# First batch's k rectified on VectorE, its transposes copied by ScalarE, epsilon added by TensorE; block 0's attends a slot up

## The chip, the cores and the metric

The kernel runs on one core of one Trainium2 chip. The metric is the device time of one execution in microseconds (us). The profile counts its own clock from the first to the last instruction (the span), which is about 1.7 us less than the run time here: the profiled run of the kernel before took 988.33 us for a span of 986.6. All stretches below are microseconds from the start of the span.

## The reference

Linear attention with a cosine feature map, followed by a layer of eight gated experts. Only the attention matters for this change.

```python
# q, k, v: 8 batches x 8 heads x 576 positions x 64
q_p = phi(q, cos_w, sin_w)      # relu(x)*cos and relu(x)*sin, side by side: 128 features
k_p = phi(k, cos_w, sin_w)
kv  = einsum('bhsf,bhsd->bhfd', k_p, v)
z   = sum(k_p, axis=2)
num = einsum('bhsf,bhfd->bhsd', q_p, kv)
den = einsum('bhsf,bhf->bhs', q_p, z)[..., None] + 1e-06
x   = num / den                 # then 4608 x 512 into the experts:
out = sum over e of P[:, e] * (relu(x @ w1[e]) @ w2[e])   # P: 8 rounds of normalised gates
```

## The kernel before

Each batch goes through these stages: rectify q and k, multiply them by the table (`q_p`, `k_p`), transpose `q_p` (batches 0 and 1 by TensorE, later ones by DMA), sum `kv` and `z`, form the denominators and their reciprocals, and "attend", which multiplies and writes the batch's part of `xT`. The first expert's two matmuls run in blocks of 512 tokens of 16 slots each (8 for `w1`, 8 for `w2`). The next batch's attention work is queued behind chosen slots with `at(block, slot, ...)`. In the traces VectorE runs its instructions in the order in which they are written. Dummy matmuls (`keep_busy`) fill TensorE's time before the first real work.

```python
qp_pool = tile_pool(name="qp_pool", bufs=3)      # the q_p buffers
rb_pool = tile_pool(name="rb_pool", bufs=4)      # reciprocals spread over partitions, for attend
# ... (cut)
def keep_busy(n):
    for _ in range(n):
        te.matmul(out=idle_ps[:, 0:P], lhsT=ones_sq[:], rhs=ones_sq[:], start=True, stop=True)

def prep_k(b, hk):
    k16 = loaded["k", b, hk]
    se.activation(out=k16, in_=k16, func=AF.Relu)

def prep_q(b, hk):
    q16 = loaded.pop(("q", b, hk))
    by_dma = b >= 2
    if by_dma:
        ve.tensor_scalar(out=q16, in0=q16, scalar1=0.0, scalar2=None, op0=ALU.max)
    q_p = qp_pool.tile([P, C, 2, D], F16, name="q_p")
    ve.tensor_tensor(out=q_p[:], in0=q16..., in1=cs, op=ALU.mult)
    if by_dma:
        qTs[b, hk] = q_pTs[(b * HK + hk) % len(q_pTs)]
        nc.sync.dma_start(out=qTs[b, hk], in_=q_p..., transpose=True)
    else:
        qps[b, hk] = q_p
# ... (cut: prep_kp makes k_p on VectorE, prep_v copies v, turn transposes on TensorE,
#      sums_begun is the kv matmuls, sums_made reads them into kv_sb and zsel)
def denominators(b):
    den_ps = ps_s.tile([P, 512], FP32, name="small_ps")
    # ... 24 matmuls zsel x q_pT into den_ps
    ve.tensor_scalar(out=den[:], in0=den_ps[0:96, 0 : C3 * HP], scalar1=1e-6 / XS, ..., op0=ALU.add)
    ve.reciprocal(out=den[:], in_=den[:])
    # ... hi and lo parts into hl, which attend spreads by matmuls
# ... (cut) the start:
for hk in range(HK):
    prep_q(0, hk)
    for i in range(3):
        turn(0, hk, i, hk < 2 or i != 1)         # True: copied by ScalarE, False: by VectorE
for hk in range(HK):
    prep_k(0, hk)
    prep_kp(0, hk)
keep_busy(30)
for half in range(2):
    prep_v(0, 2 * half, se.copy)
    prep_v(0, 2 * half + 1, ve.tensor_copy)
    begun.append(sums_begun(0, half))
    keep_busy((16, 6)[half])
sums_made(0, 0, begun[0])
sums_made(0, 1, begun[1])
denominators(0)
keep_busy(34)
# ... (cut) block 0's schedule: denominators of batch 1 at slot 9, its attends at 12 to 15,
#     batch 2's q and k preparation at 11 to 15, batch 2's last q and k at block 1
```

## Time and profile before

| | us |
|---|---|
| median of 3 runs | 986.7 (986.63 to 988.38) |
| span of the profiled run | 986.6 |
| TensorE busy | 969.7, 98% of the span |
| first attend of batch 0, 1, 2 starts at | 22.18, 43.45, 63.20 |

From the page: the span, and the first table, in which PE is TensorE, DVE VectorE, ACT ScalarE and POOL GpSimd, each with its busy time, its share of the span and its instructions.

```profile
span 986.6 us, 20264 instructions
...
PE 969.7 (98%) x7864; PEld 678.5 (69%) x7864; DVE 808.1 (82%) x1833; ACT 568.1 (58%) x1266; POOL 60.4 (6%) x82
```

TensorE is full. What there is to win lies in the first 60 us, where TensorE waits, runs dummies, or runs at half clock. The timeline of the start shows start, duration, engine, line, operation, tiles and count, and in brackets the idle time before with what ended it:

```profile
12.36 2.39 ACT L109 ACTIVATE k_ld<-k_ld 128x576 f16<-128x576 f16 x4
...
13.06 2.77 DVE L109 TENSOR_TENSOR k_p<-k_ld,acc_hi 128x1152 f16<-128x1152 f16 x4 [0.85 <-ACT k_ld L109]
...
15.36 0.46 PE L109 MATMUL small_ps<-acc_lo,k_p 64*128 64x65 f16 x18 [0.60 <-ACT acc_lo L109]
...
17.64 0.74 PE L109 MATMUL small_ps<-acc_lo,k_p 64*128 64x65 f16 x36
...
18.76 0.84 PE L109 MATMUL small_ps<-q_pT,zsel 128*32 128x192 f16 x24
19.64 0.35 DVE L109 TENSOR_SCALAR den<-small_ps 96x192 f32<-96x192 f32 x1 [0.87 <-PE small_ps L109]
20.03 1.35 DVE L109 RECIPROCAL den<-den 96x192 f32<-96x192 f32 x1
...
22.18 0.42 PE L109 MATMUL small_ps<-hl,acc_hi 96*128 96x192 f16 x3 [0.58 <-DVE hl L109]
```

Read from the top: ScalarE rectifies k late because it copies transposes first, VectorE follows with `k_p`, the kv sums (`acc_lo,k_p`) follow that, then the denominators (`zsel`), epsilon, the reciprocal, and the first attend (`hl,acc_hi`) at 22.18. The second loss is at the head of block 1, in the timeline around 50 us:

```profile
49.06 0.82 PE L109 MATMUL h_ps<-xT,w1e 128*128 128x512 f16 x3
...
50.76 0.81 DVE L109 TENSOR_TENSOR xT<-small_ps,rb 128x384 f16<-128x384 f32 x2
51.62 2.19 PE L109 MATMUL h_ps<-xT,w1e 128*128 128x512 f16 x5 [1.74 <-DVE xT L109]
...
53.75 1.17 PE L109 MATMUL small_ps<-acc_lo,k_p 64*128 64x65 f16 x36
...
63.20 0.41 PE L109 MATMUL small_ps<-hl,acc_hi 96*128 96x192 f16 x3
```

The first matmuls of block 1 wait 1.74 us for `xT`, which stands on VectorE behind work for batch 2. What comes after is slow: 36 kv sums take 1.17 us, against 0.74 in the start. The first attend of batch 2 is the line at 63.20. The table of stretches gives the reason. After each stretch's limits and length come, by engine, busy time and instructions, then the granted clock of TensorE (1.00 is full), the DMA share and GB/s:

```profile
48.33:51.74 3.41, 1.67 (x12) 0.72 (x10) 3.38 (x9) 1.77 (x4) 0.00 (x0) 1.00 1.25 163
51.74:55.15 3.41, 3.41 (x42) 1.59 (x41) 2.87 (x6) 1.39 (x4) 0.00 (x0) 0.50 1.02 205
```

The whole stretch of 3.41 us after the stall runs at half clock. The view of TensorE's waits over the first 110 us puts `xT` first:

```profile
PE h_ps L109 <- DVE xT L109: 1.9, 2, 1.7
```

### The profile page before, as it was taken

To read this page: it belongs to the slowest core of one execution; us is meant where nothing else is said; L and a number is where in the kernel's file an instruction comes from. 1 tells how busy PE (TensorE), PEld (TensorE's weight loads), DVE (VectorE), ACT (ScalarE), POOL (GpSimd) and SP (SyncE) were. 2 spreads that over 40 slices of the span, in tenths; PEclk is the share of its full clock that TensorE was granted. 3 is DMA by queue.
4 is the path that set the end of the run, shared out by engine and by line. 5 is a ranking of instruction groups with operands and counts; after the bars stand their busy time and mean duration, and the time that the engine had idled before them with its cause. 6 is when DMAs were issued, how large, how long until landed. Compare 5 with 4: busy or idle time off the path is not lost.

```text
span 986.6 us, 20264 instructions
## 1 busy us (share of the span) xinstructions
PE 969.7 (98%) x7864; PEld 678.5 (69%) x7864; DVE 808.1 (82%) x1833; ACT 568.1 (58%) x1266; POOL 60.4 (6%) x82
## 2 busy tenths in 40 slices
PE   8999999989999999999999999999999999999997
PEld 7544545447777777777777777777777777777775
DVE  6776774789889888988789888988789888988887
ACT  5756665467776555555555555555555555555551
POOL 6312110010000000000000000000000000000001
PEclk9999999999999999999999999999999999999999
DMA  9979990642013410133113400233103400104435
GB/s 166 206 108 153 160 153 20 127 75 60 26 49 68 80 36 25 41 76 68 45 29 67 92 25 26 51 65 68 49 25 67 92 25 27 48 26 114 130 86 129
DMA packets 80336, 73.54 MB, mean 75 GB/s; under 512 B 33264, under 2 KB 72176, under 8 KB 80240
## 3 DMA queue, kind: packets, MB, share of 16 engines
q0 software_dynamic: 27232, 30.94, 20.0%
q1 hardware_dynamic: 52768, 41.06, 17.1%
q8 instruction: 61, 1.00, 0.4%
q14 instruction: 35, 0.29, 0.1%
q10 hardware_dynamic: 240, 0.26, 0.1%
HBM read 83.12 MB, written 12.98 MB: 97 GB/s over the span
## 4 chain that ended last, share of the span: by engine, by line
PE 93%; DVE 3%; ACT 1%; DMA 1%; issue 1%; POOL 0%; DVEq 0%; ACTq 0%; SPq 0%; POOLq 0%
PE rows_ps L109 34%; PE h_ps L109 28%; PE copied_ps L109 11%; PE p_ps L109 11%; PE y_ps L109 5%; PE small_ps L109 4%; DMA q_pT<-q_p 1%; DVE k_p L109 0%; DVE xT L109 0%; DVE acc_hi L819 0%; POOL hs_last L834 0%; DVE P_tok L109 0%; DMA out_dram<-acc_lo 0%; ACT q_pT L109 0%; DVE colp L109 0%
## 5 line engine op out<-in xcount | busy, mean ns | idle before, releaser
L819 DVE SCALAR_TENSOR_TENSOR acc_lo<-rows_ps,P_tok,acc_lo 128x512 f32<-128x512 f32 (+1 forms) x322 | 203.4, 641 | 74.4 <-PE rows_ps L109 74.3
L109 PEld LDWEIGHTS <-H 128*128 128x128 f16 x2080 | 203.0, 98 | 83.1 <-issue 1.2
L755 ACT CAST u<-h_ps 128x384 f16<-128x384 f32 x288 | 137.8, 478 | 131.1 <-PE h_ps L109 131.1
L109 PEld LDWEIGHTS <-w1e 128*128 128x128 f16 x1632 | 156.4, 98 | 68.5 <-issue 9.0
L749 DVE CUSTOM_DVE_ANT_0 H<-p_ps,u 128x384 f16<-128x384 f32 x329 | 181.3, 551 | 6.5 <-PE p_ps L109 6.3
L109 PEld LDWEIGHTS <-hs 128*128 128x128 f16 x1500 | 146.6, 98 | 56.2
L109 PE MATMUL h_ps<-S,w1e 128*128 128x384 f16 x672 | 164.1, 326 | 1.1 <-ACT u L109 0.9
L109 PE MATMUL p_ps<-xT,T 128*128 128x384 f16 x672 | 164.1, 326 | 0.1
L109 PE MATMUL h_ps<-xT,w1e 128*128 128x384 f16 (+1 forms) x616 | 151.4, 353 | 1.9 <-DVE xT L109 1.9
L109 PE MATMUL rows_ps<-V,H 128*128 128x256 f16 x1000 | 150.0, 273 | 0.7 <-DVE acc_hi L819 0.7
L109 PE MATMUL rows_ps<-w2e,hs 128*128 128x256 f16 x1000 | 150.0, 273 | 0.0
L787 ACT ACTIVATE H<-h_ps 128x384 f16<-128x384 f32 x144 | 70.7, 491 | 95.0 <-PE h_ps L109 95.0
L109 PEld LDWEIGHTS <-T 128*128 128x128 f16 x1008 | 98.1, 98 | 29.5 <-issue 3.1
L109 PE MATMUL rows_ps<-w2e,H 128*128 128x256 f16 (+1 forms) x568 | 91.2, 285 | 0.0
L768 ACT COPY copied_ps<-h_ps 128x384 f32<-128x384 f32 x144 | 67.5, 468 | 35.4 <-PE h_ps L109 35.4
L778 ACT ACTIVATE H<-copied_ps 128x384 f16<-128x384 f32 x144 | 70.9, 492 | 20.3 <-PE copied_ps L109 20.3
L109 PE MATMUL h_ps<-S,T 128*128 128x384 f16 x336 | 81.8, 325 | 0.4 <-ACT copied_ps L109 0.3
L109 PE MATMUL copied_ps<-xT,w1e 128*128 128x384 f16 x336 | 82.1, 326 | 0.0
L109 PE MATMUL copied_ps<-w2e,H 128*128 128x256 f16 x504 | 75.5, 272 | 0.0
L109 PE MATMUL rows_ps<-V,hs 128*128 128x256 f16 x500 | 75.0, 272 | 0.0
L819 DVE SCALAR_TENSOR_TENSOR acc_lo<-copied_ps,P_tok,acc_lo 128x256 f32<-128x256 f32 x126 | 60.2, 478 | 0.6 <-PE copied_ps L109 0.2
L819 DVE SCALAR_TENSOR_TENSOR acc_hi<-rows_ps,P_tok,acc_hi 128x512 f32<-128x512 f32 (+1 forms) x56 | 41.3, 738 | 20.5 <-PE rows_ps L109 19.7
(135 smaller groups left out, 957.1 us busy)
## 6 DMA issues: line engine op xcount, KB each, us to landing
S<-x_saved SPq DMA_DIRECT2D x108, 192.0 KB, 2.4
out_dram<-acc_lo SPq DMA_DIRECT2D x62, 128.0 KB, 2.4
w1e<-in_moe_w_dram POOLq DMA_DIRECT2D x7, 1024.0 KB, 9.1
w2e<-in_moe_w_dram POOLq DMA_DIRECT2D x7, 1024.0 KB, 10.0
q_ld<-in_q_dram POOLq DMA_DIRECT2D x16, 288.0 KB, 7.7
k_ld<-in_k_dram POOLq DMA_DIRECT2D x16, 288.0 KB, 8.8
v_ld<-in_v_dram POOLq DMA_DIRECT2D x16, 288.0 KB, 10.0
x_saved<-S SPq DMA_DIRECT2D x18, 192.0 KB, 1.8
```

The costliest lines, as they stand in the source:

```text
L109: i = getattr(self.engine, name)(*args, **kwargs)
L749: latest = ve._custom_dve(TENSOR_ADD_SAT, out=out, in0=ps[:, 0:TU], in1=t[:], s0=FP32_MAX, s1=0.0)
L755: se.copy(out=t[:], in_=ps[:, 0:TU])
L768: se.copy(out=Y[:, 0:TU], in_=X[:, 0:TU])
L778: se.activation(out=h11, in_=Y[:, 0:TU], func=AF.Relu)
L787: se.activation(out=h12, in_=X[:, 0:TU], func=AF.Relu)
L819: ve.scalar_tensor_tensor(out=a, in0=rows, scalar=P_tok[:, g, self.e : self.e + 1], in1=a, op0=ALU.mult, op1=ALU.add,)
```

## The change

The intent has two parts. In the start, the first attend is to come earlier: VectorE rectifies batch 0's k as it lands, ScalarE copies all of batch 0's transposes, the first query load is issued ahead of an iota, epsilon goes into the denominators' accumulation by matmuls, and there are fewer dummies. In block 0, batch 1's attends move up a slot and part of batch 2's preparation moves to block 1, so that `xT` is in time.

```diff
+        load(0, 0, "q")
         nc.gpsimd.iota(gidx[:], ...)
-        load(0, 0, "q")
 ...
         def prep_k(b, hk):
             k16 = loaded["k", b, hk]
-            se.activation(out=k16, in_=k16, func=AF.Relu)
+            if b:
+                se.activation(out=k16, in_=k16, func=AF.Relu)
+            else:
+                ve.tensor_scalar(out=k16, in0=k16, scalar1=0.0, scalar2=None, op0=ALU.max)
 ...
+        def epsilons(b):       # three matmuls, start=True: eps_row x a row of ones into den_ps
 ...
-                turn(0, hk, i, hk < 2 or i != 1)
+                turn(0, hk, i, True)
 ...
-        keep_busy(30)
+        keep_busy(16)
         for half in range(2):
             prep_v(0, 2 * half, se.copy)
-            prep_v(0, 2 * half + 1, ve.tensor_copy)
+            prep_v(0, 2 * half + 1, (se.copy, ve.tensor_copy)[half])
             begun.append(sums_begun(0, half))
-            keep_busy((16, 6)[half])
+            keep_busy((4, 6)[half])
 ...
+        epsilons(0)
         denominators(0)        # for b == 0: no add on VectorE, the reciprocal reads PSUM
 ... block 0 (and its prep_q, turn, sums_made of batch 1 one or two slots earlier)
-                at(0, 9, denominators, 1)
-                at(0, 10, gates, 0)
+                at(0, 8, denominators, 1)
+                at(0, 9, gates, 0)
-                    at(0, 12 + hk, attend, 1, hk)
+                    at(0, 11 + hk, attend, 1, hk)
 ... block 1
-                    at(j, 0, prep_q, b, 3)
-                    at(j, 1, prep_kv, b, 3)
+                    for hk in (2, 3):
+                        at(j, 0, prep_q, b, hk)
+                        at(j, hk - 2, prep_kp, b, hk)
+                        at(j, hk - 2, prep_v, b, hk, se.copy)
 ... batch 2 in block 0: q 0 and 1, k_p 0 and 1 (v copied by ScalarE), all k rectified, slots 11 to 15
```

More of the change, by code (lines that the diff above doesn't have):

```diff
@@ L299 @@
         ve.memset(scale_row[:, 1, :], float(N) / float(E) / XS)
+        eps_row = cs_pool.tile([1, 32], FP32, name="eps_row")
+        ve.memset(eps_row[:], 1e-6 / XS)
         wg_ld = cs_pool.tile([P, KT, E], FP32, name="wg_ld")
@@ L430, in sums_made @@
                     values()
+        den_pss = {}
+        def epsilons(b):
+            den_pss[b] = ps_s.tile([P, 512], FP32, name="small_ps")
+            for j in range(3):
+                te.matmul(
+                    out=den_pss[b][32 * j : 32 * j + 32, 0 : C3 * HP],
+                    lhsT=eps_row[:],
+                    rhs=ones_col[0:1, :].to_broadcast([1, C3 * HP]),
+                    start=True,
+                    stop=False,
+                )
         def denominators(b):
             zsel = kvs[b][1]
-            den_ps = ps_s.tile([P, 512], FP32, name="small_ps")
+            den_ps = den_pss.pop(b, None)
+            if den_ps is None:
+                den_ps = ps_s.tile([P, 512], FP32, name="small_ps")
             for h in range(H):
@@ L442, in denominators @@
                         rhs=qTs[b, hk][:, j * C3 : (j + 1) * C3, hh * HP : (hh + 1) * HP],
-                        start=(h == 0),
+                        start=(h == 0 and b > 0),
                         stop=(h == H - 1),
@@ L446, in denominators @@
             den = kv_pool.tile([96, C3 * HP], FP32, name="den")
-            ve.tensor_scalar(
-                out=den[:], in0=den_ps[0:96, 0 : C3 * HP], scalar1=1e-6 / XS, scalar2=None,
-                op0=ALU.add,
-            )
-            ve.reciprocal(out=den[:], in_=den[:])
+            if b:
+                ve.tensor_scalar(
+                    out=den[:], in0=den_ps[0:96, 0 : C3 * HP], scalar1=1e-6 / XS,
+                    scalar2=None, op0=ALU.add,
+                )
+                ve.reciprocal(out=den[:], in_=den[:])
+            else:
+                ve.reciprocal(out=den[:], in_=den_ps[0:96, 0 : C3 * HP])
             hi = kv_pool.tile([96, C3 * HP], F16, name="hi")
@@ L565 @@
         prep_v(1, 3, ve.tensor_copy)
-        ahead = (
-            (prep_k, 0), (prep_q, 0), (prep_k, 1), (prep_kv, 0), (prep_q, 1), (prep_k, 2),
-            (prep_kv, 1), (prep_q, 2), (prep_k, 3), (prep_kv, 2),
-        )
         for j in range(B):
@@ L573 @@
             if j == 0:
+                at(0, 4, prep_q, 1, 0)
                 at(0, 4, lambda: begun.append(sums_begun(1, 0)))
@@ L577 @@
                 at(0, 5, lambda: begun.append(sums_begun(1, 1)))
-                at(0, 6, prep_q, 1, 0)
-                at(0, 6, lambda: sums_made(1, 1, begun[3]))
-                at(0, 6, prep_q, 1, 1)
+                at(0, 5, prep_q, 1, 1)
                 for hk in range(HK):
                     for i in range(3):
-                        at(0, 6 + hk, turn, 1, hk, i)
+                        at(0, 5 + hk, turn, 1, hk, i)
+                    if hk == 0:
+                        at(0, 5, lambda: sums_made(1, 1, begun[3]))
                     if hk < 2:
-                        at(0, 6 + hk, prep_q, 1, hk + 2)
-                at(0, 9, denominators, 1)
-                at(0, 10, gates, 0)
+                        at(0, 5 + hk, prep_q, 1, hk + 2)
+                at(0, 8, denominators, 1)
+                at(0, 9, gates, 0)
                 for hk in range(HK):
-                    at(0, 12 + hk, attend, 1, hk)
+                    at(0, 11 + hk, attend, 1, hk)
             elif b < B:
                 if j == 1:
-                    at(j, 0, prep_q, b, 3)
-                    at(j, 1, prep_kv, b, 3)
+                    for hk in (2, 3):
+                        at(j, 0, prep_q, b, hk)
+                        at(j, hk - 2, prep_kp, b, hk)
+                        at(j, hk - 2, prep_v, b, hk, se.copy)
                     at(j, 1, sums, b, 0)
@@ L605 @@
                     at(j, 3, load, b + 1, half)
-                for i, (fn, hk) in enumerate(ahead):
-                    at(j, 11 + i // 2, fn, b + 1, hk)
+                for slot, fn, hk, *args in (
+                    (11, prep_k, 0), (11, prep_q, 0), (12, prep_k, 1), (12, prep_kp, 0),
+                    (12, prep_v, 0, se.copy), (13, prep_q, 1), (14, prep_k, 2),
+                    (14, prep_kp, 1), (14, prep_v, 1, se.copy), (15, prep_k, 3),
+                ):
+                    at(j, slot, fn, b + 1, hk, *args)
             elif b + 1 < B:
```

## The prediction

> **What bounds it now.** The page has TensorE busy 98% of 986.6 us; from 100 us on the stretches table gives 877.4 busy of 886. The change touches the first 60 us. Idle there, by tens: 1.96, 1.82, 1.03, 0.59, 0.21, 1.62 us. Much "busy" before 24 us is dummy matmuls that keep the clock up, so the chain of waits prices the start: query load, transposes, k rectified on ScalarE from 12.36, four k_p on VectorE to 15.83, v copies, kv sums to 18.38, denominators to 19.6, VectorE add 0.39, reciprocal 1.36, first attend at 22.18.
> The second loss is at 49.9: block 1's first matmuls wait 1.74 us for xT, which stands on VectorE behind the third batch's work (9.08 us busy in 40-50). The granted clock is then 0.50 from 51.9 to 55.1, about 1.6 us more. [...]
>
> **What changes.**
> 1. The first query load is issued before the iota: about 0.5 us earlier. DMA is saturated (about 205 GB/s), so later landings move no more than that.
> 2. ScalarE takes two more transpose copies (0.49 each) and no k; VectorE rectifies k (that form on q lasts 0.30; ScalarE's 0.6) as it lands (halves at about 10.1 and 12.5). k_p ends near 14.1. Then v's second half (about 15.0) limits. With 12 fewer dummies before the second half, the sums end near 16.0, not 18.38.
> 3. Epsilon by three fp32 matmuls: 0.39 leaves VectorE, about as much TensorE time comes in: nearly nothing. Fewer dummies may leave the clock at 0.5 for sums and denominators: minus up to 1 us.
> So the first attend starts near 20.0: 2.0 to 2.5 us gained.
> 4. Second batch's denominators and attends a slot up, two of the third batch's queries and keys to block 1, its v copies to ScalarE (0.67 against 0.45). The 1.74 us wait and most of the cold clock go: up to 3.4 us. ScalarE is then nearly full at 41-48: minus 0.5.
>
> **What gives some back.** The third batch's queries are transposed by DMA while loads still run: the load issued at 40.26 took 11.8 us to land, the first transpose 8.7. Data moves at most 0.5 us earlier, the work 5 to 6. The four transposes can hardly land before 55 (estimate: 0.9 MB left at 52, at 0.27 MB/us). The third batch's denominators, which ended at 60.2, would come at 53 and must wait, ending near 56. Some 1.7 of the 5.5 us gained stay in that new wait.
>
> **Prediction.** Net about 3.8 us, all on the critical path: **983.0 us**, 80% range 980.8 to 985.6. Faster by over 2%: 0.01; within 2%: 0.98; slower: 0.01.
>
> **What would show it.** Timeline: last kv sum of batch 0 near 16, first attend near 20. Waits of TensorE: h_ps for xT falls from 1.9 us to under 0.5; a new wait of small_ps (third batch's denominators or sums) for the DMA transposes or k_p, 1 to 3 us, near 50-56. From 60 us on the same work, shifted.
>
> **What would make it wrong.** If transposes share the DMA better, the gain is 5 to 6 us. If a q_p buffer waits for a starved transpose, VectorE stops in order, k_p too, and the clock falls again: gain 1 to 2. A cold clock through the first denominators costs 1 us.

One sentence, on what brings the half clock about, is cut from this text: no trace or run of this case shows it. No term of the forecast's sum goes with it (5.5 us gained, less 1.7, is the net of 3.8). That dummies keep the clock up was measured later: with 48 of them ahead of batch 0's sums the clock was 1.00 through the start (b1_fill), with 16 it was 0.50 from 15.7 to 22.5 (after). In the trace of before a stretch at 0.50, from 10.80 to 14.21, lies under dummies all the same.

## The result and the profile after

The changed kernel took a median of 986.46 us (four runs, 985.85 to 987.01) against 986.75 (four runs, 986.63 to 988.38). Ratios here are the mean time of one kernel's fast runs over that of the other's of the same rounds, so not quite the ratio of the medians quoted: 0.9993, with a 95% interval of 0.9976 to 1.001. That is the same time, outside the predicted range of 980.8 to 985.6.

Intervals are about 1.2 to 1.7 us wide to each side, so single timings hardly separate these kernels. The kernel before alone spreads from 986.17 to 989.11 over later rounds. What follows therefore rests on milestones in the traces: the start of the first attend of batches 0, 1 and 2, and the span. From batch 2's first attend to the end, all traces take 922.6 to 923.1 us, except that of the kernel before (923.4, which holds one wait of 0.46 for `xT` at 89.2).

| trace | batch 0 | batch 1 | batch 2 | span |
|---|---|---|---|---|
| before | 22.18 | 43.45 | 63.20 | 986.6 |
| after | 23.16 | 43.69 | 61.89 | 984.8 |

From the page of the changed kernel:

```profile
span 984.8 us, 20226 instructions
...
PE 969.9 (98%) x7844; PEld 678.4 (69%) x7844; DVE 805.8 (82%) x1830; ACT 568.6 (58%) x1269; POOL 60.6 (6%) x82
```

The span is 1.8 us shorter, but the profiled run of the kernel before was a slow one: it took 988.33 us, and three of that kernel's four timed runs took 986.63 to 986.79 (the fourth 988.38). The timeline of the start:

```profile
10.12 0.31 DVE L109 TENSOR_SCALAR k_ld<-k_ld 128x576 f16<-128x576 f16 x1 [0.25 <-DMA k_ld<-in_k_dram]
...
14.60 1.03 PE L109 MATMUL small_ps<-acc_lo,k_p 64*128 64x65 f16 x36 [2.13 <-ACT acc_lo L109]
...
15.37 0.67 ACT L109 COPY acc_lo<-v_ld 128x576 f16<-128x576 f16 x1 [0.24 <-DMA v_ld<-in_v_dram]
...
16.09 1.17 PE L109 MATMUL small_ps<-acc_lo,k_p 64*128 64x65 f16 x36
...
17.94 0.86 PE L109 MATMUL small_ps<-ones_col,eps_row 1*32 1x192 f32 x6
...
18.73 1.47 PE L109 MATMUL small_ps<-q_pT,zsel 128*32 128x192 f16 x24
...
20.25 1.35 DVE L109 RECIPROCAL den<-small_ps 96x192 f32<-96x192 f32 x1 [2.62 <-PE small_ps L109]
...
23.16 0.41 PE L109 MATMUL small_ps<-hl,acc_hi 96*128 96x192 f16 x3
```

VectorE now rectifies k at 10.12, as soon as it lands, and the second kv sums start 1.55 us earlier than before (16.09 against 17.64). But TensorE stands idle for 2.13 us ahead of the first sums, because there are fewer dummies to cover that stretch. The second sums then take 1.17 instead of 0.74, and the denominators 1.47 instead of 0.84. The epsilon matmuls add 0.86 (the trace counts each of the three as two). The whole lead is gone by the reciprocal, which starts at 20.25 against 20.03. The stretches show the clock:

```profile
13.00:14.00 1.00, 0.00 (x0) 0.00 (x0) 0.94 (x2) 0.12 (x1) 0.70 (x1) 1.00 1.25 199
16.00:17.00 1.00, 1.00 (x36) 0.97 (x36) 0.08 (x1) 0.42 (x3) 0.42 (x2) 0.50 1.34 206
21.00:22.00 1.00, 1.00 (x12) 1.00 (x11) 0.93 (x3) 0.00 (x0) 0.71 (x1) 0.50 1.20 199
```

It is full while TensorE idles, then 0.50 from 15.7 to 22.5. The copy of v's second half starts at 15.37, as soon as it landed, and ends at 16.04, just ahead of the second sums at 16.09. The head of block 1 did what was hoped:

```profile
50.34 1.90 PE L109 MATMUL h_ps<-xT,w1e 128*128 128x512 f16 x8
...
52.17 0.74 PE L109 MATMUL small_ps<-acc_lo,k_p 64*128 64x65 f16 x36
...
58.52 0.35 PE L109 MATMUL small_ps<-q_pT,zsel 128*32 128x192 f16 x6 [0.52 <-DMA q_pT<-q_p]
...
61.89 0.41 PE L109 MATMUL small_ps<-hl,acc_hi 96*128 96x192 f16 x3
```

The eight matmuls of the first slot run without a gap and at full clock. There is one new wait, 0.52 us for a transpose by DMA. TensorE's waits over the first 110 us:

```profile
PE small_ps L109 <- ACT acc_lo L109: 2.1, 1, 2.1
...
PE small_ps L109 <- DMA q_pT<-q_p: 0.5, 1, 0.5
...
PE h_ps L109 <- DVE xT L109: 0.2, 1, 0.2
```

The wait of `h_ps` for `xT` fell from 1.9 to 0.2. So the two traces say that the start became about 1.0 us later, and that the stretch from batch 0's first attend to batch 2's became 2.3 us shorter (38.73 against 41.02).

### The profile page after: what moved, and what is told of

Its sections match the earlier page's. It is cut to its first block, busy times and chain, and to the rows that moved or that the text cites. A ratio compares the mean times of both kernels' runs of the same rounds, so it can differ in the third digit from the quotient of the medians.

```text
span 984.8 us, 20226 instructions
## 1 busy us (share of the span) xinstructions
PE 969.9 (98%) x7844; PEld 678.4 (69%) x7844; DVE 805.8 (82%) x1830; ACT 568.6 (58%) x1269; POOL 60.6 (6%) x82
## 4 chain that ended last, share of the span: by engine, by line
PE 94%; DVE 2%; DMA 2%; ACT 1%; POOL 1%; issue 0%; POOLq 0%; ACTq 0%; SPq 0%
PE rows_ps L109 34%; PE h_ps L109 28%; PE copied_ps L109 11%; PE p_ps L109 11%; PE y_ps L109 6%; PE small_ps L109 4%; DMA v_ld<-in_v_dram 1%; DMA q_pT<-q_p 0%; DVE acc_hi L847 0%; POOL hs_last L862 0%; DVE P_tok L109 0%; DMA out_dram<-acc_lo 0%; DVE colp L109 0%; ACT u L109 0%; POOL k_ld L201 0%
```

## The experiments

All thirteen kernels gave correct results and were timed in five rounds. "Median" is the kernel's; the ratio is to the kernel before in the same rounds. No ratio of a pair of edited kernels was measured. Such pairs are compared by milestones of one trace each, so a difference of a few tenths between single traces is not much.

The theory was that the start lost its gain to half clock, caused by TensorE's idle time ahead of the sums. The rivals were the epsilon matmuls, DMA contention, and that block 1's stall was never worth what the trace of the kernel before said.

### First group: again, and the two parts alone

**a0_before and a1_after**: the two kernels unchanged.

> The unchanged kernel once more, for the noise and for a second trace. Theory P [...] the profiled run of before was an unlucky one (its run took 988.38 us where the other three took 986.63 to 986.79). Then this trace has a span near 985.0, and less time at half clock than the 3.4 us at 10.9 to 14.3 plus 3.2 us at 51.9 to 55.1 of the first trace. Rival: those two stretches belong to the kernel; then both are there again and the span is 986.6. Ratio to before 1.000 either way.

Measured: median 987.03, ratio 0.9999 (0.9986 to 1.0012). Milestones 23.97, 45.24, 63.47, span 986.4. The expected span near 985.0 was missed; the expected smaller time at half clock came (one stretch of 3.4 us in place of two). The same kernel gave a different trace: its start ran at half clock from 16.4 to 19.8, under the second half of the sums and the dummies between, and its first attend came 1.8 us later than in the first trace. Ahead of the sums TensorE stood idle for 1.79 us, which was 0.60 in the first trace. The stall came too, in the timeline:

```profile
15.85 0.46 PE L109 MATMUL small_ps<-acc_lo,k_p 64*128 64x65 f16 x18 [1.79 <-ACT acc_lo L109]
...
53.41 1.24 PE L109 MATMUL h_ps<-xT,w1e 128*128 128x512 f16 x5 [1.74 <-DVE xT L109]
...
54.58 0.74 PE L109 MATMUL small_ps<-acc_lo,k_p 64*128 64x65 f16 x36
```

The same 1.74 us wait, but no half clock behind it: the sums take 0.74. From batch 0's attend to batch 2's took 39.50, not 41.02. So the cold clock behind the stall, 1.5 us, is a thing that some executions have and others don't.

> The changed kernel once more, second trace. Theory C (cold start): TensorE idles 2.1 us ahead of the first kv sums because of the fewer dummies, and the sums, the epsilon and the denominators run at half clock (15.9 to 22.7 in the first trace); it is there again[...] and the first attend is near 23 us again, not near 20. Rival: it was bad luck[...]; then the first attend comes at 21 to 22. Ratio to before 0.9985 to 1.000.

Measured: median 986.73, ratio 0.9992 (0.9979 to 1.0006). Milestones 23.30, 44.03, 62.10, span 985.0: the changed start repeats its late attend.

**a2_block**: the kernel before with the change's schedule of blocks 0 and 1 alone.

```diff
 # on the kernel before: start, epsilon, load order and dummies as before; only
-                at(0, 9, denominators, 1)
+                at(0, 8, denominators, 1)
 # ... and the rest of the hunks from there on (attends a slot up, batch 2's work later)
```

> Only the part of the change in blocks 0 and 1 (second batch's attends a slot up, third batch's work later, its v copies on ScalarE); the start is that of before. If the wait of 1.74 us for xT near 50 us and the half clock after it are a loss of every run of before, this saves 1.5 to 3 us: 983.7 to 985.3, ratio 0.997 to 0.9985, better than the whole change. If the wait is only regained at the DMA transposes, the wait of TensorE for q_pT grows to 1.5 us or more and the ratio is 0.9985 to 1.0.

Measured: median 986.39, ratio 0.9985 (0.9973 to 0.9998). Milestones 22.22, 42.77, 60.96, span 983.6. The measured ratio is the weak end of what was expected. The block part alone takes 38.74 from batch 0's to batch 2's attend and keeps the earlier start.

**a3_start**: the complement, the changed start with the schedule of before.

```diff
 # on the changed kernel
-                at(0, 8, denominators, 1)
+                at(0, 9, denominators, 1)
 # ... and the rest of the schedule back as it was before
```

> Only the part of the change at the start (load ahead of iota, k rectified on VectorE, all copies of the transposes on ScalarE, fewer dummies, epsilon on TensorE); blocks 0 and 1 are those of before. Theory C: half clock through sums and denominators, first attend 0.5 to 1.5 us later than 22.18, time 986.8 to 988.3, ratio 1.0 to 1.0015. Rival (the start saves what was predicted and block 0 gives it back): first attend near 20, ratio below 0.999.

Measured: median 987.17, ratio 0.9994 (0.9981 to 1.0007). Milestones 23.06, 44.52, 62.75, span 985.5. Again a late start, at half clock from 16.8 to 23.5; the ratio lies just under the expected 1.0 to 1.0015. Again the 1.74 us stall (ended at 52.69) without half clock after it, and 39.69 from batch 0's to batch 2's attend.

What follows: the changed start gives 23.06 to 23.30 in three traces; the start of before gives 22.18, 22.22 or 23.97. It is not earlier. The block part is worth 38.7 against 39.5 and 39.7, so 0.8 to 1.0 us, where the stall is not followed by half clock, and 2.3 where it is.

### Second group: the idle stretch and epsilon

**b1_fill**: the changed kernel with the idle stretch filled by dummies.

```diff
-        keep_busy(16)
+        keep_busy(48)
-            keep_busy((4, 6)[half])
+            keep_busy((10, 6)[half])
```

> The changed kernel with the idle time of TensorE ahead of the first kv sums filled: 48 dummies there in place of 16, 10 in place of 4 between the halves. Theory C (the half clock at the start ate the gain): no half clock between 15 and 23 us, sums, epsilon and denominators last 0.74, 0.43 and 0.84 us in place of 1.17, 0.86 and 1.47, the first attend is at 21.0 to 21.8 in place of 23.2, and if nothing later gives it back the time is 1.5 us below the changed kernel's. Theory D (a floor by the DMA transposes of the third batch): the first attend comes earlier all the same, but TensorE's wait for q_pT near 58 us grows from 0.5 to 1.5 us or more, and the third batch's first attend stays near 61.9. Rival to C: the clock is low for another reason, and the attend stays at 23.

Measured: median 987.13, ratio 0.9989 (0.9975 to 1.0003). Milestones 20.97, 41.51, 63.26, span 986.2. Timeline of the start:

```profile
10.95 2.84 PE L109 MATMUL y_ps<-ones_sq 128*128 128x128 f16 x48
...
16.24 0.74 PE L109 MATMUL small_ps<-acc_lo,k_p 64*128 64x65 f16 x36
...
17.35 0.52 PE L109 MATMUL small_ps<-ones_col,eps_row 1*32 1x192 f32 x6
17.81 0.84 PE L109 MATMUL small_ps<-q_pT,zsel 128*32 128x192 f16 x24
...
20.97 0.42 PE L109 MATMUL small_ps<-hl,acc_hi 96*128 96x192 f16 x3 [0.32 <-DVE hl L109]
```

With the stretch filled, sums, epsilon and denominators run at full clock and the first attend comes 2.2 us earlier than in the changed kernel. The half clock was the cause of the failed start. All traces agree: where TensorE idled for 1.67 to 2.13 us ahead of the first sums (after, a1_after, a3_start, b2_eps, and a0_before with no edit at all), the clock fell by the second half of the sums; where it idled for at most 0.81 us (the other ten), it stayed full there. But batch 2's attend is at 63.26, later than in the changed kernel: the start's gain was lost again, and more. Timeline at 54 us:

```profile
54.07 0.76 DVE L109 TENSOR_TENSOR q_p<-q_ld,acc_hi 128x1152 f16<-128x1152 f16 x1 [2.74 <-DMA q_pT<-q_p]
54.74 0.75 DVE L109 TENSOR_TENSOR k_p<-k_ld,acc_hi 128x1152 f16<-128x1152 f16 x1
...
55.55 0.60 PE L109 MATMUL small_ps<-acc_lo,k_p 64*128 64x65 f16 x18 [2.60 <-DVE k_p L109]
```

There are three `q_p` buffers, and the fourth `q_p` of batch 2 waits for the first one's transpose. VectorE works in order, so the next `k_p` stands behind it, and TensorE waits 2.60 us for that. The view of transfers gives the time from issue to landing of the transpose issued in 44 to 45:

```profile
q_pT<-q_p SPq DMA_TRANSPOSE x1, 9.3
```

In the same trace the loads' queue moved 176 packets and the transposes' 51 in the stretch 48 to 49, and 34 and 299 in 51 to 52. So both queues progress side by side, and most of the transposes' packets move only as the loads run out. Then the clock fell as well, from 55.7 to 59.1, in the table of stretches:

```profile
57.00:58.00 1.00, 1.00 (x4) 0.36 (x3) 0.00 (x0) 0.00 (x0) 0.00 (x0) 0.50 1.04 233
```

**b2_eps**: the changed kernel with epsilon back on VectorE, nothing filled.

```diff
-        epsilons(0)
         denominators(0)     # start=(h == 0) and the VectorE add, for every batch
```

> The changed kernel with epsilon added by VectorE again, as before; the dummies of the change. If the three fp32 matmuls cost what they last (0.86 us at half clock) and VectorE's add 0.39, the first attend comes 0.3 to 0.5 earlier, at 22.7. If those matmuls[...] the clock comes back [...]at 19.3 in place of 22.7, and the attend is at 21.8 to 22.3.

The cut clauses gave a reason for an earlier return of the clock. No run shows it. Measured: median 985.93, ratio 0.9982 (0.997 to 0.9995). Milestones 21.85, 42.39, 61.36, span 984.2. The clock fell at the same place, 15.8, but came back at 19.2, one stretch earlier, so the attends ran at full clock:

```profile
18.00:19.00 1.00, 1.00 (x24) 0.88 (x18) 0.00 (x0) 0.00 (x0) 0.71 (x1) 0.50 1.20 204
20.00:21.00 1.00, 1.00 (x22) 1.00 (x19) 1.00 (x1) 0.00 (x0) 0.25 (x1) 1.00 1.20 210
```

**b3_fill_eps**: both edits together.

```diff
 # b1_fill's dummies, and as in b2_eps
-        epsilons(0)
```

> Both: the idle time filled, and epsilon on VectorE. Theory C: full clock, first attend at 20.8 to 21.6. If epsilon by TensorE is worth nothing at full clock either, the same attend as with the filled one alone, within 0.2. Theory D: third batch's first attend still near 61.5 to 62 and a wait for q_pT of 1.5 us or more; against D: it moves with the first attend, to 60.

Measured: median 986.8, ratio 0.9986 (0.9974 to 0.9999). Milestones 20.74, 41.28, 62.19, span 985.1. Half clock from 55.8 to 59.1, as in b1_fill, and TensorE's wait was again for `k_p` (1.80 us), not for `q_pT` as theory D had it. At full clock it is not worth having the epsilon on TensorE: 20.74 without, 20.97 with. That 0.23 us is one trace each; what is safe is that the matmuls gave nothing.

### Third group: the transposes' give-back

These build on b3_fill_eps.

**c1_bufs**: a fourth `q_p` buffer. One `rb` buffer was given up for it.

```diff
-        qp_pool = ... bufs=3
+        qp_pool = ... bufs=4
-        rb_pool = ... bufs=4
+        rb_pool = ... bufs=3
```

> The filled start with epsilon on VectorE, and four buffers for q_p in place of three (three for rb in place of four make the room). Theory D': with the early start VectorE stands 2 to 3 us at the fourth q_p of the third batch, because the first one's transpose by DMA (9.3 us to land) still holds one of three buffers, and k_p behind it holds up TensorE. With a fourth buffer that wait is gone; TensorE waits for the transposes themselves, at the third batch's denominators, 1 to 3 us. Third batch's first attend at 59.5 to 61, time 0.5 to 2 us below the filled kernel. Rival: the buffer is not what holds it, and k_p is as late as before.

Measured: median 985.2, ratio 0.9981 (0.9969 to 0.9993), against 987.96 for the kernel before in its rounds. Milestones 20.89, 41.43, 60.89, span 983.6. No half clock anywhere in the first 66 us. VectorE no longer waits for a buffer. What is left is three short waits for transposes, in TensorE's waits from 36 to 70:

```profile
PE small_ps L109 <- DMA q_pT<-q_p: 1.5, 3, 0.6
```

**c2_kfirst**: both `k_p` of block 1's start ahead of the fourth `q_p`, with three buffers.

```diff
+                    at(j, 0, prep_q, b, 2)
                     for hk in (2, 3):
-                        at(j, 0, prep_q, b, hk)
                         at(j, hk - 2, prep_kp, b, hk)
                         at(j, hk - 2, prep_v, b, hk, se.copy)
+                    at(j, 1, prep_q, b, 3)
```

> The filled start with epsilon on VectorE, and the third batch's last k_p ahead of its last q_p on VectorE. Theory D': the kv sums no longer wait for the buffer (the wait of TensorE for k_p, 1.8 us, goes), but the last q_p and its transpose are as late as before, so TensorE waits 2 to 3 us for q_pT at the denominators instead; third batch's first attend 61 to 62.5, time as the filled kernel's within 1 us.

Measured: median 986.29, ratio 0.9985 (0.9973 to 0.9997). Milestones 20.87, 41.42, 62.14, span 985.1. The wait for `k_p` is gone, but two waits for transposes (1.1 us, less than the 2 to 3 expected) remain, and the clock fell from 57.8 to 61.3. In its trace it gains nothing over b3_fill_eps, which also has a half-clock stretch. The 1.25 us by which c1_bufs' trace is ahead at batch 2 go with that stretch, and the timed runs do not show that the buffer prevents it: see "Which runs kept their clock" below.

**c3_hold**: the loads of q for batch 3 held back, so that they should not stand beside batch 2's transposes.

```diff
-                    at(1, 0, load, b + 2, half)
+                    at(1, 0, load, b + 2, half, "kv")
+                for half in range(2):
+                    at(1, 1, load, b + 2, half, "q", True)    # held back: after VectorE's last
```

> The filled start with epsilon on VectorE, and the fourth batch's two query loads held back until VectorE has begun block 1's work. Theory D: those 0.6 MB (2.8 us of the DMA at the 1.4 us a load takes) stood ahead of the transposes; they land that much earlier, the wait for k_p or q_pT near 54 to 58 falls below 0.7 us, there is no half clock after it, the third batch's first attend is at 58.8 to 60 and the time is 1.5 to 2.5 us below the filled kernel (ratio 0.9965 to 0.998 to before). Against D: waits as before.

Measured: median 988.05, ratio 1.0007 (0.9995 to 1.0019). Milestones 20.47, 41.02, 63.23, span 986.3. The expectation fell: holding loads back until VectorE was done only moved them beside the last transpose. GpSimd issued them at 51.94:

```profile
51.94 1.43 POOL L201 DMA_DIRECT2D q_ld<-in_q_dram  x2 [13.21 <-DVE q_p L109]
```

TensorE then waited once for the transpose, for 3.0 us, in its waits from 36 to 70:

```profile
PE small_ps L109 <- DMA q_pT<-q_p: 3.0, 1, 3.0
```

**c4_bufs_hold**: c1_bufs and c3_hold together.

```diff
 # c1_bufs' pools with c3_hold's loads
```

> Both: four q_p buffers, and the fourth batch's query loads held back. If one of the two is enough, as with the better of them alone, within 0.5 us. Third batch's first attend at 58.5 to 59.5, no wait over 0.6 us of TensorE between 25 and 62, ratio to before 0.9965 to 0.998.

Measured: median 988.21, ratio 1.0001 (0.9988 to 1.0014). Milestones 20.91, 41.45, 64.44, span 987.1, with a wait of 3.7 us for the last transpose, where none over 0.6 had been expected. Holding back spoils the fourth buffer's gain.

### Fourth group: what the start's parts are worth

These build on c1_bufs, in whose trace the clock stays full.

**d1_relu**: batch 0's k rectified on ScalarE again and v's first half split over both engines again, with more dummies to keep the stretch filled.

```diff
-            if b:
+            if True:
                 se.activation(out=k16, in_=k16, func=AF.Relu)
-        keep_busy(48)
+        keep_busy(68)
-            prep_v(0, 2 * half + 1, (se.copy, ve.tensor_copy)[half])
+            prep_v(0, 2 * half + 1, ve.tensor_copy)
```

> The filled kernel with four q_p buffers, and k of the first batch rectified by ScalarE again (v copies as before; 68 dummies in place of 48 to cover the longer gap). If rectifying on VectorE is what brings the start forward once the clock is full, the last kv sums of batch 0 start at 16.8 to 17.3 in place of 16.35 and the first attend is at 21.3 to 22.0 in place of 20.9. If the filled clock alone does it, the attend stays within 0.2 of 20.9. The time then hardly tells, as the third batch's transposes take up to 1 us of it: ratio to before 0.9975 to 0.999.

Measured: median 986.26, ratio 0.999 (0.9975 to 1.0004). Milestones 22.41, 42.95, 61.58, span 984.5. The first attend comes 1.5 us later than in c1_bufs (20.89), with full clock in both. That is a little later than expected (21.3 to 22.0). So rectifying on VectorE, together with v's first half on ScalarE, is worth about 1.5 us of the start; this run does not separate the two. The number of dummies differs too, but TensorE still idles for 0.22 us between them and the first sums, so they did not hold these up.

**d2_order**: the first query load behind the iota again.

```diff
-        load(0, 0, "q")
         nc.gpsimd.iota(...)
+        load(0, 0, "q")
```

> The filled kernel with four q_p buffers, and the first query load behind the iota again. By the prediction's step 1 it lands 0.5 us later and the attend moves by as much. By the traces since (the second half of v lands at 15.2 to 15.5 in all six, whatever the order) nothing moves: first attend within 0.3 of 20.9, ratio within 0.0008 of the same kernel with the load ahead (0.998).

Measured: median 986.9, ratio 0.9994 (0.9981 to 1.0006). Milestones 20.47, 41.01, 60.91, span 983.5. With the old order the attend is if anything earlier (20.47 against 20.89). The load order gave nothing. Its median lies above c1_bufs' by 1.7 us although the traces are alike. The traced run was the fastest of its five (985.21) and the only one with a mean granted clock of 0.999; the other four had 0.997 or 0.998. So this trace, without half clock, does not stand for the kernel's usual run.

| trace | batch 0 | batch 1 | batch 2 | span | half clock, 10 to 110 us |
|---|---|---|---|---|---|
| a2_block | 22.22 | 42.77 | 60.96 | 983.6 | 11.1 to 14.4 |
| b1_fill | 20.97 | 41.51 | 63.26 | 986.2 | 55.7 to 59.1 |
| b2_eps | 21.85 | 42.39 | 61.36 | 984.2 | 15.8 to 19.2 |
| c1_bufs | 20.89 | 41.43 | 60.89 | 983.6 | none |
| c2_kfirst | 20.87 | 41.42 | 62.14 | 985.1 | 57.8 to 61.3 |
| d1_relu | 22.41 | 42.95 | 61.58 | 984.5 | none |

**Which runs kept their clock.** The record has the mean granted clock of every timed run of the changed kernel and of the experiments, not only of the traced ones. One half-clock stretch of 3.41 us in 985 lowers the mean by 0.0017, so a run at 0.999 or 1.000 has no room for a whole one.

| kernel | runs at 0.999 or 1.000 | their spans |
|---|---|---|
| before | 8 of 43 | 984.6 to 985.1 |
| changed, unedited | 1 of 9 | 984.0 |
| three `q_p` buffers (b3_fill_eps, c2_kfirst) | 5 of 11 | 983.1 to 984.1 |
| four `q_p` buffers (c1_bufs, d2_order) | 5 of 10 | 983.2 to 983.6 |

With the clock kept, the changed kernel's one run is 0.6 to 1.1 us ahead of the kernel before, not 3.8. And in these few runs the fourth buffer shows no effect on how often the clock is kept (c1_bufs 4 of 5, d2_order 1 of 5).

## Why the prediction was wrong

The prediction summed 2.0 to 2.5 us (start) plus up to 3.4 (block 1's head), less 0.5 and less 1.7, to a net of 3.8. Measured net: 0.3 in the medians. Point by point:

1. **"So the first attend starts near 20.0: 2.0 to 2.5 us gained." This step failed.** It started at 23.16, 23.30 and 23.06. The term that was mis-sized is the one before it, "Fewer dummies may leave the clock at 0.5 for sums and denominators: minus up to 1 us". b1_fill measured it: 2.2 us (23.16 to 20.97, one trace each; the filled starts of the later runs repeat it). The prediction named the danger, but sized it at half or less of what it cost and left "near 20.0" standing, and it did not see that the clock would stay down for two stretches and through the attends' start (15.7 to 22.5). Even at full clock the attend was at 20.97, not 20.0. Of that 1.0, all lies before the end of the sums ("near 16.0", measured 16.98 in b1_fill): v's second half is copied from 15.34 to 16.01, the ten dummies in between end at 16.30, and 0.74 us of sums come after that. From there to the attend the prediction allowed 4.0 and b1_fill took 3.99.

2. **"about 0.5 us earlier" for the query load: failed.** The load was issued at 1.30 instead of 1.40, the second query load at 2.62 instead of 2.53 and v's loads at 5.31 instead of 4.90, in the timelines of GpSimd, which issues them. d2_order shows no gain from the new order.

3. **Epsilon on TensorE, "nearly nothing": right at full clock, wrong in the kernel as changed.** b1_fill against b3_fill_eps is 20.97 against 20.74, with 0.52 us of epsilon matmuls. Where the clock is down it cost more: 0.86 us of matmuls, and the clock came back one stretch later than without them (b2_eps: 19.2, not 22.5), together 1.3 us of the first attend (23.16 against 21.85, one trace each). This overlaps with the 2.2 of point 1 and is not added to it.

4. **Rectifying k on VectorE: the mechanism was right.** With v's first half on ScalarE it is worth about 1.5 us (d1_relu against c1_bufs), once the clock is kept.

5. **"The 1.74 us wait and most of the cold clock go: up to 3.4 us": the mechanism was right, the size was not.** The wait went (1.9 to 0.2), and the cold clock of that trace went. But one block 0 matmul group of about 0.87 us only moved from before the attends to after them, small waits grew or came (0.42 for `zsel` and 0.41 for a transpose's copy, where the kernel before has two of 0.3, and 0.52 for a DMA transpose), and the cold clock is one that only some executions of the kernel before have. Two traces (a0_before, a3_start) show the same stall without it. Where it is absent, the part is worth 0.8 to 1.0 us. The prediction took one trace's cold clock, and that of a slow run, for a property of the kernel.

6. **The give-back, "Some 1.7 of the 5.5 us gained stay in that new wait": right in kind.** In the changed kernel it was only 0.52 us, as the start was not early. When the start was made early, the give-back took everything in b1_fill's trace. That is the mechanism listed under what would make the prediction wrong: a `q_p` buffer waiting for a starved transpose, VectorE stopping in order, and the clock falling again. c1_bufs removed the buffer's wait: three waits of 1.5 us in all remain in its trace, close to the 1.7. That it also keeps the clock is not shown (four buffers: 5 of 10 runs, three: 5 of 11).

Why the medians differ by only 0.3 is less sure than the above. An estimate from the traces: an execution of the kernel before with its early start (22.2) and without cold clock behind the stall (39.5, then 922.9) has a span of 984.6, or a run of about 986.3 us. The changed kernel's own sum is 23.2 + 38.7 + 922.9 = 984.8. They are alike, as measured. No trace shows such an execution of before, but the record has eight timed runs of it at a granted clock of 1.000, with spans of 984.6 to 985.1. Half clock at the start is not the whole reason, though: the one run of the changed kernel that kept its clock has a span of 984.0, and b1_fill's one has 984.2. As far as the traces show, the rest of the predicted 3.8 us is the cold clock of the first trace counted as gain (point 5), and what an early start gives back (point 6); no run separates the two shares.

**What decides between cold and warm is not shown.** The half-clock stretches in the table and the timelines above last about 3.4 us or twice that (3.41 each in before, 6.83 in after), and they do not stand at the same place in each execution: they begin at 10.80 and 51.74 in one trace of the kernel before and at 16.4 in the other. With them the first attend came at 22.18 and 23.97 for the same code. Beyond the idle time ahead of the first sums (1.67 us and more against 0.81 and less), no run shows what sets where such a stretch begins. How often the clock was kept: see the table of runs above.

**The better version.** c1_bufs, with the stretch filled, epsilon on VectorE and four `q_p` buffers, has the best median (985.2) and a ratio of 0.9981 (0.9969 to 0.9993), so about 1.9 us faster than the kernel before. It was picked after the fact, and its lead over the other edited kernels is not shown: b2_eps has 0.9982 (0.997 to 0.9995), and d2_order, the same kernel but for the load order, 0.9994. It was compared with the kernel before, not with the changed kernel directly. Its trace's milestones are 2.3 and 1.0 us ahead of the changed kernel's at batches 0 and 2.

## What to carry to other kernels

Shortening what runs ahead of a wait can leave the tensor engine idle, and half clock after the idle time may cost more than was saved (here 2.2 us, after against b1_fill), so refill the gap that a change opens with dummies before judging it. A stall's after-effects in one trace (a cold clock above all) may belong to that execution (1.5 us in the trace of before, none in a0_before): take a second trace of the same kernel before counting them as gain. And work that arrives earlier meets whatever was hidden behind it: count the buffers that a slower transfer keeps, because an engine that works in order carries the wait to everything behind (2.74 us on VectorE in b1_fill).

## What the traces show of the clock and the transposes

- Stretches in which TensorE was partly busy went ahead of a loss of clock. In the 3.41 us before the clock fell it was busy for 1.67 us in the trace of before (48.33 to 51.74), and in the 3.43 us before it fell for 2.27 us in c2_kfirst (54.40 to 57.83).
- Busy time over such a stretch does not tell the cases apart: in a0_before a stretch of 3.41 us around the same stall was also 1.67 us busy and the clock stayed. Its limits are the author's estimate, carried on in steps of 3.41 us from the change of clock at 16.4 in that trace; no run shows over which time the clock is decided. That stretch held wide matmuls after the stall. Whether the shape of the matmuls matters was not tested.

```profile
50.53:53.94 3.41, 1.67 (x10) 0.70 (x8) 3.38 (x8) 1.49 (x5) 0.00 (x0) 1.00 0.97 153
```

- The return to full clock took different times. In a1_after TensorE was busy for the whole of the first stretch shown here, with some ten dummies, the one-row epsilon matmuls and the 32-column denominators, and the clock stayed at half for the next stretch too. The same holds in after (half clock from 15.7 to 22.5) and a3_start (16.8 to 23.5). Without epsilon on TensorE the clock was back after one stretch, in two traces (b2_eps, 15.8 to 19.2; a0_before, 16.4 to 19.8).

```profile
16.96:20.37 3.41, 3.41 (x43) 2.29 (x42) 0.88 (x3) 0.43 (x2) 1.90 (x3) 0.50 1.21 206
20.37:23.78 3.41, 3.41 (x33) 3.23 (x30) 1.47 (x3) 0.00 (x0) 1.43 (x2) 0.50 1.32 201
```

- A transpose that stands beside loads took 9.3 us from issue to landing (b1_fill) and 8.7 (before), where the median of the transposes in the trace of before is 3.9.
